# Attention and a squared-ReLU layer in one program: the first product of blocks 4 to 11 taken two blocks at a time, in a new written order

## Chip, cores and metric

One core of a Trainium2 chip runs the whole program in one launch. The metric is device time in microseconds (us). The kernel before took 197.66 us (median of 3 runs, 197.29 to 197.74).

## What is computed

The reference is local attention with a few global keys, followed by a feed-forward layer with a squared ReLU:

```
scores = (q @ k.T) / 8 - slope[h] * dist          # 4 batches, 8 heads, 768 positions, 64 wide
keep   = (key < 8) | (0 <= query - key < 96)      # 8 global keys, 96 local ones
a      = softmax(where(keep, scores, -1e9))
x      = (a @ v), heads side by side              # 3072 tokens x 512
h      = x @ w_in                                 # 512 x 2048
out    = (relu(h) ** 2) @ w_out                   # 2048 x 512
```

## The kernel before

**Tiles and blocks.** The 3072 tokens are 24 tiles of 128, numbered 0 to 23, six to a batch. Two tiles make a block, 0 to 11. The attention goes tile by tile, the feed-forward layer block by block. TensorE, VectorE, ScalarE, GpSimd and SyncE are called PE, DVE, ACT, POOL and SP, as in the profile.

**Attention of a tile j** (names as in the written order below): `load.j.1` brings q and k, `load.j.0` brings v (POOL issues them; for the tiles 0 to 5 they are single loads `ld.q.j`, `ld.k.j`, `ld.v.j`). `T.j` turns q and k: by PE (`tr`) and a copy up to tile 7, by a DMA transpose from SP from tile 8 on. `sc.j` are the scores on PE (L621). `exp.j.odd.g` are four exponentials of 128x512 on ACT (two for the first tile of a batch, L687); `mul.j.g` multiplies them by the bias on DVE (L712); `pv.j.0` and `pv.j.1` are the weighted sums of v on PE (L774); `norm.j` divides by the row sums, once for a tile, on DVE (L808, L809); `xT.j` turns the result, by PE (`trx`) up to tile 7, by a DMA transpose from SP (L894) after that.

**First product of a block** (`h`, PE, L1019). It is a Strassen-like product of seven parts, `p1` to `p7`. `xs` (DVE, L988) makes the differences of x that three of the parts need, `isum` those of w_in. Block 0 is not done so (`s1`, L1140), and of block 1 only the second half is. The parts go to three PSUM banks: x takes p1, p6, p7, p4 in this order, y takes p2, z takes p5 and p3. Between two parts on a bank its content is copied out (`u`, mostly ACT, L450) or summed and clipped at zero (`c`, DVE, L1064, or a plain ReLU on ACT, L919), since the next part adds onto the bank. `q` squares the result (ACT L1086, or DVE L1088). A part is 8 matmuls of 128 columns: four steps of the hidden dimension by two of the model dimension, and the four results fill a bank of 4x128 columns.

**Second product of a block** (`s2`, PE, L1279) is of seven parts too, each in two halves of four matmuls of 256 columns. `sum` (DVE, L1234) makes the sums of the hidden values that it needs, `wsum` (DVE, L1199) those of w_out, `part` (ACT, L450) copies between parts, `o` (DVE, L1354, or ACT) makes the output rows, and `st` stores them from SP. The second half of the first part, `s2.0.p1.1`, needs the last four of the eight loads of w_out.

**The order is written out by hand.** A string ORDER lists all operations; each engine takes its own in that order, in-order. A word names the operation, the PSUM banks or buffers that it takes (behind `:`), and at times the engine (`@A`, `@V`). Waits follow from data and from the buffers named. All loads by POOL run through one queue, in the order of the string. The constants that the change touches, and the lines that use the first of them:

```
L271      PAIRS = ()
L955          blks = (blk, blk) if mate is None else (blk, mate)
L956          wide = mate is not None
L957          GRP = 2 if wide else 4
L958          W = 2 * P if wide else P
...
                    for n, s in enumerate(range(GRP * g, GRP * g + GRP)):
                        for k in range(2):
                            nc.tensor.matmul(
                                out=tiles["h", blk, g, bank][:, n], lhsT=left_[:, s, k], rhs=right_[:, k],
...
L1120             if s == 0 and blk not in [z[0] for z in PAIRS]:
L1121                 pair = [z for z in PAIRS if z[1] == blk]
L1122                 if pair:
L1123                     first_seven(pair[0][0], mate=blk)
L1124                 else:
L1125                     first_seven(blk)
```

With `mate` given, the two halves of the tokens that the seven parts combine are the two blocks themselves instead of the two tiles of one block. A matmul then has 256 columns instead of 128, a part does two hidden steps instead of four, and there are four groups `h.b.0` to `h.b.3` for the pair instead of two for each block. `xs` takes both of its buffers for a pair, and each of its four operations is one of 128x512 values; for a block alone there is one of 128x512 and two of 128x256.

Of the kernel before, what the change touches and what calls it, by code (L numbers as in the profile page):

```python
# [57 lines left out]
tr.0.0:0 tr.1.0:1 bias.0.0:23 T.0.0 ld.q.2 tr.0.2:0 ld.q.1 tr.0.1:4 T.1.0@A sc.0.0 T.0.2 ld.k.1 tr.1.1:0 T.1.1  # L58
bias.1.0:1567 exp.0.0.0:0 ld.k.2 T.0.1@A tr.1.2:0 sc.1.0 exp.0.1.0 T.1.2 exp.1.1.0:1 gk.1 exp.1.0.1:3 exp.1.1.1
exp.1.0.0 bias.2.0:3420 sc.2.0 ld.q.3 gk.2 exp.2.1.1:2 ld.v.0 pv.0.0:56 pv.0.1 tr.0.3:7 exp.2.0.1 exp.2.0.0:0 norm.0:0  # L60
ld.v.1 ld.k.3 tr.1.3:1 T.0.3 T.1.3 pv.1.0:56 pv.1.1 exp.2.1.0 norm.1:1 sc.3.0:1372 gk.3 exp.3.1.1:3 exp.3.1.0:1
exp.3.0.0 ld.k.4 tr.1.4:4 T.1.4 exp.3.0.1 ld.q.4 tr.0.4:0 trx.0:5 T.0.4 sc.4.0:0426 exp.4.0.1:4 xT.0:0 mul.3.0:5 gv.1
exp.4.1.1 mul.3.1:1 ld.k.5 tr.1.5:1 T.1.5 exp.4.1.0:6 ld.v.2 pv.2.0:23 pv.2.1 trx.1:6 ld.q.5 tr.0.5:7 T.0.5@A gk.4
exp.4.0.0 norm.2:0 trx.2:2 gv.2 ld.v.3 pv.3.0:34 pv.3.1 sc.5.0:0715 xT.1@A ld.win.1.0 s1.0.1:6 xT.2:1 s1.0.1#2 norm.3:0
trx.3:3 ld.win.3.0 s1.0.3:4 s1.0.3#2 exp.5.1.1:1 gv.3@A ld.v.4 E0.1 ld.win.2.0 xT.3 s1.1.1:3 exp.5.0.1 exp.5.0.0:5
relu.0.3:2 mul.4.1:0 s1.0.2:0 mul.4.0:3 pv.4.0:45 pv.4.1 E0.0 exp.5.1.0 ld.win.2.1 gv.4@A relu.0.1:0 s1.0.2#2 s1.1.3:7
relu.1.3:3 sq.0.1:0 mul.5.1:6 s1.1.2:1 norm.4:0 gate.11 trx.4:4 ld.win.0.0 xT.4@A:2 ld.v.5 s1.0.0:7 ld.win.0.1 s1.0.0#2
s1.0.0#3 s1.0.2#3 mul.5.0:1 relu.1.1:0 ld.win.6.0 ld.win.7.0 isum.0.0 ld.win.5.0 xs.1.0:0 relu.1.2:5 pv.5.0:56 xs.1.1
isum.1.0 s1.0.0#4 relu.0.0:1 sq.0.3 ones.6 pv.5.1 norm.5:0 s1.0.2#4 h.2.0.p1:3 u.2.0.1:6 relu.0.2:2 sq.1.3:1 isum.2.0
sq.0.2 h.2.0.p2:1 gate.9 c.2.0.c11:4 s1.0.7:7 relu.0.7:3 isum.3.0 trx.5:5 xT.5 xs.2.0:1 ld.win.4.0 isum.0.1 xs.2.1  # L70
xs.1.2 isum.1.1 s1.0.6:6 relu.0.6:2 xs.2.2 s1.0.5:1 relu.0.5:6 h.1.1.p1:7 u.1.1.1:7 ld.wout.1 isum.3.1 h.2.1.p2:6
ld.wout.2 ld.wout.0 ld.wout.3 h.2.1.p1:5 sq.0.0 u.2.1.1:8 c.2.1.c11:1 h.1.1.p2:1 c.1.1.c11:9 sq.0.6 h.2.0.p6 u.2.0.2:a
sq.0.7 s1.0.4:0 relu.0.4@V:8 ld.wout.7 ld.wout.6 ld.wout.4 sq.0.5 isum.2.1 h.1.1.p6 u.1.1.2:3 sq.0.4 wsum.0.0 sum.0.0:0
sum.0.1 gate.12 s1.1.0:6 h.2.1.p6 u.2.1.2:6 h.2.0.p5:0 sq.1.2 h.2.0.p7 h.1.1.p7 h.1.1.p5:1 h.2.1.p7 s2.0.p2.0:4 wsum.1.0
u.2.0.3:8 h.2.0.p4 c.2.0.c22:5 u.1.1.3:7 c.1.1.c22:2 sq.1.1 u.2.1.3:b relu.1.0:8 sq.1.0 h.1.1.p4 h.2.1.p5:2 c.2.0.c21:7
wsum.2.0 c.2.1.c22:0 h.1.1.p3 c.1.1.c12:8 h.2.0.p3 ld.wout.5 wsum.0.1 wsum.2.1 wsum.1.1 h.2.1.p4 s2.0.p1.0:3 s2.0.p1.1
wsum.3.0 s2.0.p2.1 q.1.1.c22 load.6.1 tr.1.6:1 tr.0.6:6 h.2.1.p3 sum.0.2 c.2.1.c12:2 gate.10 q.1.1.c11 part.0.p1:0
load.6.0 c.1.1.c21:9 q.1.1.c12 q.2.0.c11:2 s2.0.p6.0 s2.0.p6.1 part.0.p6:1 o.0.p2:4 s2.1.p1.0:7 T.0.6@A s2.1.p1.1
q.2.0.c22 part.1.p1:0 wsum.3.1 s2.0.p7.0 s2.0.p7.1 c.2.0.c12:6 T.1.6 load.7.1 sum.0.3 s2.0.p5.0 tr.1.7:6 tr.0.7:2
s2.0.p5.1 part.0.p7:2 c.2.1.c21:5 s2.0.p4.0 s2.0.p4.1 o.0.p5:a s2.0.p3.0 s2.0.p3.1 sum.1.0:1 sum.1.1 q.2.1.c11  # L80
q.1.1.c21@V T.1.7@A sum.1.2 sum.1.3 T.0.7@A o.0.p4 q.2.0.c12 q.2.1.c12 sc.6.0:326510 exp.6.0.0:2 exp.6.1.0 s2.1.p6.0
s2.1.p6.1 mul.6.0:9 o.0.p3 part.1.p6:2 s2.1.p2.0:3 s2.1.p2.1 o.1.p2:2 s2.1.p7.0 s2.1.p7.1 load.8.1 exp.7.1.1:6 exp.7.0.1
mul.7.1:1 pv.6.0:01 pv.6.1 gk.7@A exp.7.0.0:8 s2.1.p5.0 load.7.0 s2.1.p5.1 part.1.p7:0 s2.1.p4.0 exp.7.1.0 q.2.1.c22
gate.13 load.9.1 T.8 sc.8.0:5642 exp.8.0.1:0 norm.6:0 T.9 mul.7.0:6 pv.7.0:01 pv.7.1 o.1.p5:9 s2.1.p3.0 s2.1.p3.1
exp.8.1.1 load.8.0 load.10.1 load.9.0 T.10 exp.8.0.0:1 exp.8.1.0 trx.6:4 load.11.1 xT.6@A:2 s2.1.p4.1 o.1.p4 sum.2.0:0
norm.7:1 trx.7:5 xT.7@A gk.8 o.1.p3 sc.9.0:3012 exp.9.0.0:6 h.3.1.p1:4 h.3.0.p1:7 exp.9.1.0 mul.8.1:8 mul.8.0:3 gv.7
pv.8.0:56 pv.8.1 s2.2.p1.0:3 exp.9.0.1:1 exp.9.1.1 h.3.0.p2:0 sum.2.1 xs.3.0:1 xs.3.1 norm.8:1 xT.8:1 mul.9.0:8
h.3.1.p2:1 s2.2.p1.1 mul.9.1:3 T.11 u.3.0.1:0 h.3.0.p6 sum.2.2 u.3.1.1:b h.3.1.p6 xs.3.2 c.3.1.c11:1 gk.9 part.2.p1:2
s2.2.p6.0 gv.8@A pv.9.0:56 pv.9.1 norm.9:0 xT.9 u.3.1.2:6 u.3.0.2:c s2.2.p6.1 q.2.1.c21 h.3.1.p7 u.3.1.3:5 part.2.p6:0
c.3.0.c11:b h.3.0.p7 sc.10.0:5612 exp.10.0.1:0 exp.10.1.1 exp.10.1.0:3 h.3.1.p5:0 h.3.1.p4 exp.10.0.0 u.3.0.3@V:8  # L90
h.3.0.p4 q.2.0.c21@V q.3.0.c11:1 c.3.1.c22:d h.3.0.p5:1 s2.2.p2.0:2 s2.2.p2.1 gv.9 mul.10.1:5 c.3.1.c21:0 mul.10.0:7
h.3.1.p3 s2.2.p7.0 c.3.0.c22:b c.3.1.c12:3 o.2.p2:8 c.3.0.c21:e q.3.0.c22 q.3.1.c11 load.10.0 pv.10.0:45 pv.10.1
h.4.1.p1:7 h.3.0.p3 load.12.1 gk.10@A q.3.1.c22 u.4.1.1:1 s2.2.p7.1 norm.10:1 s2.2.p5.0 sum.2.3 T.12 c.3.0.c12:d
# [72 lines left out]
def kernel(  # L166
# [98 lines left out]

    SETS = {}
    JOIN = {(7, 0), (13, 0), (19, 0)}
    COPY = []
    BEHIND = {}
    WHOLE = True  # L270
    PAIRS = ()  # L271
    NHB = 4
    NXT = 4
    SEVEN = set(range(NBLK))
    SEVEN1 = set(range(2, NBLK))
    SEVEN1_PART = {(1, 1)}
    GRP = 4
# [1221 lines left out]
```

## Time and profile before

| | |
|---|---|
| profiled execution, its own time | 197.03 us |
| its span, first to last instruction | 195.3 us |
| granted PE clock | 1.00 |
| busy in the span: PE, DVE, ACT, POOL | 188.3, 177.0, 158.6, 75.1 us |
| bytes moved by DMA | 26.92 MB |

The profile page gives busy time for each engine, a chain of the work that ended last (followed back from the last instruction to what released each step), and groups of instructions by source line. A matmul's recorded end includes the pipeline, so PE can be shown busy while it waits some tenths of a microsecond; the distance from one group of matmuls to the next in the chain is the better measure. The chain's rows have a start, a length and what ran; the timeline's rows have a start, a length, engine, line, operation, tiles, count and, in brackets, the idle time before and what ended it.

### The profile page before, as it was taken

The numbers are of one execution on the slowest core, as the hardware profiler recorded it, in microseconds if no ns is written. First come the engines' busy times: TensorE is split into PE (matmuls) and PEld (weight loads), VectorE is DVE, ScalarE is ACT, GpSimd is POOL, SyncE is SP. The second block draws the span as 40 slices with busy tenths as digits, with TensorE's granted clock in tenths as the row PEclk, the third lists the DMA queues.
The fourth block names the chain that finished last, engine by engine and source line by source line (L and its number), as shares of the span: only waits on it lengthen the run. The fifth ranks groups of instructions, "written<-read, shape, count | busy, mean of one in ns | idle before, by whom it ended". The sixth has DMA issues, their size and how long they took to land.

```text
span 195.3 us, 6863 instructions
## 1 busy us (share of the span) xinstructions
PE 188.3 (96%) x2808; PEld 171.1 (88%) x2808; DVE 177.0 (91%) x395; ACT 158.6 (81%) x331; POOL 75.1 (38%) x93
## 2 busy tenths in 40 slices
PE   7986999999999999999999999999999999999993
PEld 3865999999889989989989999998888999999882
DVE  8478999999999999999999999978999999998960
ACT  6798899999989897999997968675987979666511
POOL 8999965747575039056230009290000000000000
PEclk9999999999999999999999999999999999999999
DMA  8999999999999999999999349999855402100055
GB/s 130 149 155 174 177 201 202 204 159 158 179 159 126 147 161 191 136 240 135 142 240 84 77 91 104 198 171 206 166 104 118 134 5 57 54 3 0 0 192 187
DMA packets 111713, 26.92 MB, mean 138 GB/s; under 512 B 103234, under 2 KB 108866, under 8 KB 111682
## 3 DMA queue, kind: packets, MB, share of 16 engines
q0 software_dynamic: 80256, 13.37, 91.9%
q1 hardware_dynamic: 31426, 13.11, 32.2%
q8 instruction: 22, 0.36, 0.7%
q14 instruction: 9, 0.07, 0.1%
HBM read 27.26 MB, written 6.29 MB: 172 GB/s over the span
## 4 chain that ended last, share of the span: by engine, by line
PE 82%; DVE 10%; ACT 3%; DMA 2%; issue 1%; ACTq 0%
PE bank L1019 32%; PE bank L1279 32%; PE bank L1140 5%; PE bank L621 5%; PE bank L774 4%; DVE x L809 2%; DVE hsum L1234 2%; DMA xT<-x 2%; PE bank L393 2%; DVE buf L712 2%; PE bank L531 2%; ACT early L687 1%; ACT buf L687 1%; DVE xs L988 1%; DVE early L712 1%
## 5 line engine op out<-in xcount | busy, mean ns | idle before, releaser
L1279 PEld LDWEIGHTS <-hsum 128*128 128x128 bf16 x384 | 35.9, 98 | 3.9
L450 ACT COPY buf<-bank 128x512 f32<-128x512 f32 (+1 forms) x56 | 30.8, 564 | 10.0 <-PE bank L1019 5.8
L1279 PE MATMUL bank<-wsum,hsum 128*128 128x256 bf16 x288 | 37.7, 273 | 0.0
L687 ACT ACTIVATE buf<-bank 128x512 bf16<-128x512 f32 x54 | 30.1, 604 | 2.3 <-PE bank L621 2.3
L1019 PEld LDWEIGHTS <-qk_first 128*128 128x128 bf16 x504 | 30.7, 98 | 1.4 <-DVE xs L988 0.3
L1086 ACT ACTIVATE hs<-buf 128x512 bf16<-128x512 f32 x46 | 28.7, 636 | 3.5 <-DVE buf L1064 3.2
L1019 PEld LDWEIGHTS <-win 128*128 128x128 bf16 x504 | 30.8, 98 | 0.8
L1064 DVE CUSTOM_DVE_ANT_0 buf<-bank,buf 128x512 f32<-128x512 f32 x42 | 28.3, 684 | 1.8 <-ACT early L687 0.7
L1279 PEld LDWEIGHTS <-hs 128*128 128x128 bf16 x288 | 26.7, 98 | 2.7
L331 POOL DMA_DIRECT2D qk<-in_q_dram x18 | 16.0, 889 | 30.1 <-DMA qkT<-qk 25.7
L1279 PE MATMUL bank<-wout,hs 128*128 128x256 bf16 x192 | 26.0, 273 | 0.0
L1019 PE MATMUL bank<-xT,win 128*128 128x128 bf16 x336 | 24.3, 219 | 0.0
L1019 PE MATMUL bank<-xs,qk_first 128*128 128x128 bf16 x336 | 24.1, 219 | 0.2 <-DVE xs L988 0.2
L331 POOL DMA_DIRECT2D v<-in_v_dram x18 | 16.1, 898 | 20.5 <-DVE hsum L1234 14.3
L687 ACT ACTIVATE early<-bank 128x512 bf16<-128x512 f32 x34 | 19.2, 612 | 2.8 <-PE bank L621 2.7
L809 DVE TENSOR_TENSOR x<-bank,rs 128x512 bf16<-128x512 f32 x24 | 16.6, 692 | 0.9
L331 POOL DMA_DIRECT2D qk<-in_k_dram x18 | 16.2, 898 | 2.3 <-DMA wout<-in_moe_w_out_dram 2.3
L1234 DVE TENSOR_TENSOR hsum<-hs 128x1024 bf16<-128x1024 bf16 (+1 forms) x26 | 16.7, 643 | 0.0
L450 ACT COPY part<-bank 128x256 f32<-128x256 f32 x31 | 11.6, 376 | 5.8 <-PE bank L1279 5.6
L1354 DVE TENSOR_TENSOR buf<-bank,part 128x256 f32<-128x256 f32 x29 | 12.1, 419 | 3.6 <-PE bank L1279 3.3
L621 PEld LDWEIGHTS <-qkT 64*128 64x128 bf16 x352 | 10.0, 94 | 3.9 <-issue 2.6
L1279 PE MATMUL bank<-wout,hsum 128*128 128x256 bf16 x96 | 13.3, 273 | 0.0
(93 smaller groups left out, 379.8 us busy)
## 6 DMA issues: line engine op xcount, KB each, us to landing
out_dram<-buf SPq DMA_DIRECT2D x17, 256.0 KB, 2.5
v<-in_v_dram POOLq DMA_DIRECT2D x24, 128.0 KB, 5.6
qk<-in_q_dram POOLq DMA_DIRECT2D x18, 128.0 KB, 4.8
qk<-in_k_dram POOLq DMA_DIRECT2D x18, 128.0 KB, 5.4
wout<-in_moe_w_out_dram POOLq DMA_DIRECT2D x8, 256.0 KB, 10.2
win<-in_moe_w_in_dram POOLq DMA_DIRECT2D x6, 256.0 KB, 6.7
out_dram<-early SPq DMA_DIRECT2D x5, 256.0 KB, 2.8
qk_first<-in_q_dram POOLq DMA_DIRECT2D x5, 128.0 KB, 4.4
```

The lines of the kernel that those rows point to most:

```text
L331: nc.gpsimd.dma_start(out=dst, in_=src)
L450: nc.scalar.copy(dst, src)
L621: nc.tensor.matmul(out=tiles["sc", j, odd, g][:, at, :], lhsT=left[j - 1][half, pair, :] if kt else qkT[j % NKT][half, 1, pair, :], rhs=qk ...
L687: nc.scalar.activation(out=tiles[tag, j, g][:, odd], in_=tiles.pop(("sc", j, odd, g)).rearrange("p a c -> p (a c)"), func=Act.Exp, scale=s ...
L809: nc.vector.tensor_tensor(out=x.rearrange("p (b a) c -> p b a c", b=2), in0=po[:, :, :, :D], in1=rs.to_broadcast([P, 2, 4, D]), op=Alu.mult,)
L1019: nc.tensor.matmul(out=tiles["h", blk, g, bank][:, n], lhsT=left_[:, s, k], rhs=right_[:, k], start=opens and n == 0 and k == 0, stop=k == ...
L1064: nc.vector._custom_dve(TENSOR_ADD_SAT, out=hr, in0=src, in1=tiles.pop(("u", blk, g, i)), s0=float("inf"), s1=0.0,)
L1086: nc.scalar.activation(hs, hr, Act.Square)
L1140: nc.tensor.matmul(out=hT[:, c, cols], lhsT=w_in_sb[s][:, kt, c * P : (c + 1) * P], rhs=tiles["xT", blk][:, kt, cols], start=(kt == 0), st ...
L1234: nc.vector.tensor_tensor(out=t[:, i, h], in0=t[:, a, h] if isinstance(a, int) else half_a(blk, *a)[:, h], in1=t[:, b, h] if isinstance(b, ...
L1279: nc.tensor.matmul(out=tiles["acc", blk, bank][:, cols], lhsT=left_[:, s], rhs=right_[:, cols], start=first and s == 0, stop=s == NSTEP - ...
L1354: nc.vector.tensor_tensor(out=o_sb[:, cols], in0=tiles["acc", blk, bank][:, part], in1=tiles["part", blk, other][:, part], op=Alu.add,)
```

## The change

Two things change: the constant PAIRS, and the whole ORDER string. PE transposes up to tile 7 and one normalisation for a tile stand in both kernels.

```diff
-    PAIRS = ()
+    PAIRS = ((4, 5), (6, 7), (8, 9), (10, 11))
```

Of the string, the line before and the line after at the place where block 0 begins its second product:

```diff
-sum.0.1 gate.12 s1.1.0:6 h.2.1.p6 u.2.1.2:6 h.2.0.p5:0 sq.1.2 h.2.0.p7 h.1.1.p7 h.1.1.p5:1 h.2.1.p7 s2.0.p2.0:4 wsum.1.0
+exp.6.1.0 h.2.0.p3 exp.7.0.1:2 c.2.0.c12:b h.2.0.p2:1 s2.0.p1.0:7 exp.7.1.1 exp.7.1.0 h.2.0.p4 c.2.0.c21:8 ld.wout.7 T.8
```

**PE, the first part of the first product of block 4.** Before, 128 columns to a matmul (`xT_107` is the turned x of block 4, `win` the weights):

```order
L1019 LDWEIGHTS win
L1019 MATMUL bank<-xT_107,win 128x128
L1019 LDWEIGHTS win
L1019 MATMUL bank<-xT_107,win 128x128
L1019 LDWEIGHTS win
L1019 MATMUL bank<-xT_107,win 128x128
```

Now:

```order
L1019 LDWEIGHTS win
L1019 MATMUL bank<-xT_107,win 128x256
L1019 LDWEIGHTS win
L1019 MATMUL bank<-xT_107,win 128x256
L1279 LDWEIGHTS hsum_114
L1279 MATMUL bank<-wsum_91,hsum_114 128x256
```

Each weight load now serves 256 columns, four in a part instead of eight, and a part of block 2's second product follows.

**POOL, the queue of loads, from the last loads of w_in on.** `qk_67` to `qk_69` are the q and k of the tiles 6, 8 and so on, `v_77` is the v of tile 6. Before:

```order
L327 DMA win<-in_moe_w_in_dram 128x4x256 x4
L327 DMA wout<-in_moe_w_out_dram 128x2x512 x8
L331 DMA qk_67<-in_q_dram 128x8x64
L331 DMA qk_67<-in_k_dram 128x8x64
L331 DMA v_77<-in_v_dram 128x8x64
```

Now:

```order
L331 DMA qk_67<-in_q_dram 128x8x64
L331 DMA qk_67<-in_k_dram 128x8x64
L327 DMA win<-in_moe_w_in_dram 128x4x128 x2
L327 DMA win<-in_moe_w_in_dram 128x4x256
L331 DMA qk_69<-in_q_dram 128x8x64
L331 DMA qk_69<-in_k_dram 128x8x64
L327 DMA wout<-in_moe_w_out_dram 128x2x512
L331 DMA qk_68<-in_q_dram 128x8x64
L331 DMA qk_68<-in_k_dram 128x8x64
L327 DMA wout<-in_moe_w_out_dram 128x2x512 x3
L331 DMA qk_67<-in_q_dram 128x8x64
L331 DMA qk_67<-in_k_dram 128x8x64
```

Behind these stand the last four loads of w_out and then `v_77`:

```order
L327 DMA wout<-in_moe_w_out_dram 128x2x512 x4
L331 DMA v_77<-in_v_dram 128x8x64
L331 DMA qk_68<-in_q_dram 128x8x64
L331 DMA qk_68<-in_k_dram 128x8x64
L331 DMA v_78<-in_v_dram 128x8x64
```

Eight loads, q and k of the tiles 6, 8, 7 and 9, have moved ahead of the last loads of w_out; the v of tile 6 stands behind all of them as it did behind w_out before.

**ACT, around the first exponentials of tile 6** (L687 are exponentials, `part` the copies between parts of the second product, `hs` the squares). Before:

```order
L450 COPY part_129<-bank 128x256
L919 ACTIVATE buf_122<-bank 128x512
L1086 ACTIVATE hs_111<-buf_121 128x4x128
L1086 ACTIVATE hs_112<-buf_117 128x4x128
L450 COPY part_130<-bank 128x256
L450 COPY qkT_86<-bank 128x512
L1086 ACTIVATE hs_112<-buf_118 128x4x128
L450 COPY part_129<-bank 128x256
L450 COPY part_131<-bank 128x256
```

Now:

```order
L1176 ACTIVATE hs_111<-early 128x512 x2
L687 ACTIVATE early<-bank 128x512 x6
L919 ACTIVATE buf_121<-bank 128x512
L687 ACTIVATE buf_120<-bank 128x512
L1086 ACTIVATE hs_111<-buf_118 128x4x128
L687 ACTIVATE buf_120<-bank 128x512
L687 ACTIVATE buf_118<-bank 128x512
L450 COPY part_129<-bank 128x256
```

Nine exponentials of the tiles 6 to 8 now stand ahead of the first copy of the second product (`part_129`). Before, the four copies shown (`part_129` twice, `part_130`, `part_131`) stood ahead of the first exponential of tile 6, which came some rows behind them.

206 lines of the change are left out of this document (103 added, 103 removed).

## Prediction

> **What bounds the kernel now.** I read the page first, then the chain of waits in order of time, the stages of the span, and the queue of loads.
>
> ```profile
> PE 188.3 (96%) x2808; PEld 171.1 (88%) x2808; DVE 177.0 (91%) x395; ACT 158.6 (81%) x331; POOL 75.1 (38%) x93
> ...
> PE 82%; DVE 10%; ACT 3%; DMA 2%; issue 1%; ACTq 0%
> ```
>
> PE carries 82% of the chain, but DVE and ACT have little to spare. Where they have least, the stages show (columns: PE, PEld, DVE, ACT, POOL busy, clock, DMA, GB/s):
>
> ```profile
> 10.00:20.00 10.00, 7.71 (x165) 6.22 (x164) 8.04 (x23) 8.64 (x19) 10.00 (x14) 1.00 2.13 165
> ...
> 20.00:58.30 38.30, 38.30 (x564) 35.49 (x561) 37.82 (x83) 36.29 (x76) 25.59 (x32) 1.00 1.81 181
> ...
> 170.00:180.00 10.00, 10.00 (x131) 9.38 (x129) 9.23 (x18) 7.27 (x16) 0.00 (x0) 1.00 0.06 23
> ```
>
> Up to 20 us everything still waits for the first loads. From 20 to 58.3 us three engines are full together: DVE idles 0.48 us (38.30 - 37.82) and ACT 2.01 us. Later ACT has over a quarter to spare. The chain says the same: from 47 to 64.5 us it runs through DVE, after that through PE almost alone.
>
> ```profile
> 47.78 0.41 DVE buf L1354
> ...
> 56.99 0.01 DVE early L1354
> ...
> 60.98 1.20 DVE buf L712 x2
> ...
> 64.56 0.62 PE bank L621 x16
> ...
> 77.60 1.34 PE bank L1019 x24
> ...
> 179.82 12.24 PE bank L1279 x112
> 192.08 0.37 ACT buf L450
> ```
>
> So what shortens PE's work counts only if nothing puts PE later in the first 60 us; and what puts it later there is not won back, because behind that PE has no idle time to win it from.
>
> **The change, term by term.** The sum is made against the profiled execution, 197.03 us (span 195.3 us and 1.73 us around it). It stands 0.63 us below the median of the runs, 197.66 us, and I add that at the end.
>
> *PE's work.* A part of the first product is 8 matmuls of 128 columns now and 4 of 256 afterwards. The chain has both back to back: 24 of 128 in 1.34 us, 55.8 ns each, 0.447 us a part; 112 of 256 in 12.24 us, 109.3 ns each, 0.437 us a part. Four pairs by four groups by seven parts are 112 parts: 112 x 0.0095 = **-1.06 us**. All of it is on the path, since PE is. The halved weight loads (448 fewer) take nothing off besides, since they lie beside the matmuls.
>
> ```profile
> L1019 PEld LDWEIGHTS <-win 128*128 128x128 bf16 x504 | 30.8, 98 | 0.8
> ```
>
> A load lasts 98 ns by itself, and yet 128-column matmuls follow one another every 55.8 ns. The Trainium skill (TensorE: Matmul & The Clock Gate, Back-to-back issue gap) gives some 81 ns for a sustained stream of weight loads and 128-column matmuls. By that price a part of eight would be 0.65 us and the change would take off some 24 us, an estimate from that section; the chain's 55.8 ns speaks against it, and the sum goes by the chain.
>
> *xs on DVE.* For two blocks alone it is two of 128x512 and four of 128x256, for a pair four of 128x512.
>
> ```profile
> L988 DVE TENSOR_TENSOR xs<-xT,xs 128x256 bf16<-128x256 bf16 x22 | 6.2, 284 | 0.3
> L988 DVE TENSOR_TENSOR xs<-xT 128x512 bf16<-128x512 bf16 x11 | 4.6, 419 | 0.3 <-DMA xT<-x 0.3
> ```
>
> 4 x 0.419 against 2 x 0.419 + 4 x 0.284: 0.30 us less a pair, 1.2 us in all. It falls behind 58 us, where DVE is not what PE waits for, so I cost it at nothing. If DVE were still the bound there, it would be a gain of up to 1.2 us. The copies, sums and squares keep their number and size; DVE gives four squares to ACT, hidden in ACT's idle time late in the span.
>
> *The first 60 us in the new order.* The first product of block 4 now needs the tiles 8 to 11 and not 8 and 9, so attention is pulled ahead of the second products. Three floors follow, and the highest counts.
>
> (a) *Loads.* In the order of before, the last load of w_out is issued at 30.48 us; the queue is full, each issue waiting for a landing.
>
> ```profile
> 26.44 0.70 POOL L327 DMA_DIRECT2D wout<-in_moe_w_out_dram  x1 [0.52 <-DMA win<-in_moe_w_in_dram]
> ...
> 30.48 0.71 POOL L327 DMA_DIRECT2D wout<-in_moe_w_out_dram  x1 [0.67 <-DMA win<-in_moe_w_in_dram]
> DMA to landing us min/median/max: 8.9/10.2/10.8
> q0 software_dynamic: 10893, 1.38, 217.0%
> L331 POOL DMA_DIRECT2D v<-in_v_dram x18 | 16.1, 898 | 20.5 <-DVE hsum L1234 14.3 <-DVE v L501 6.2
> ```
>
> The third row is that of w_out's tile: it lands at 39.4 to 41.3 us. The fourth is the queue from 40 to 50 us: 1.38 MB in 10 us, so 128 KB take 0.95 us; by POOL's own row an issue is 0.90 us. Eight loads of q and k now stand ahead, and the v of tile 6 follows: nine by 0.90 to 0.95 make that v land at 47.5 to 49.9 us, middle 48.7. PE's first use of it is the weighted sum of tile 6, which before ran here:
>
> ```profile
> 52.76 0.41 PE L774 MATMUL bank<-v,buf 128*128 128x65 bf16 x8
> ...
> 57.86 1.07 PE L1019 MATMUL bank<-xT,win 128*128 128x128 bf16 x16
> ```
>
> Counted in both orders, the work of PE ahead of it is the same but for 16 halves of second products fewer (16 x 0.437 = 6.99 us) and one group of scores more (0.62 us, the 16 matmuls of L621 in the chain above). PE would come to it at 52.76 - 6.37 = 46.4 us. It waits **1.1 to 3.5 us**, middle 2.3. In-order, everything of PE is queued behind it: the rest of blocks 0 and 1's second products and the scores of tile 9, and ACT and DVE behind these.
>
> (b) *ACT.* A place with the same work of PE ahead of it in both orders (to 0.2 us) is the first part of block 3. Before, it is the second half of the row at 57.86, at 58.3 us. Ahead of it ACT must now have done 39 exponentials instead of 32, and with the smaller differences 3.4 us more:
>
> ```profile
> 14.49 0.99 ACT early L687 x2
> ...
> 57.51 0.43 ACT L450 COPY buf<-bank 128x256 f32<-128x256 f32 x1
> ```
>
> 7 x 0.50 us are 3.5; the rest cancels. The copy at 57.51 us is ACT's last operation that this place needs, in both orders. With all 2.01 us of idle time used, it comes at 57.51 + 3.4 - 2.0 = 58.9 us and lasts 0.43 us, so the place is at 59.3 us; without waits PE would be there at 58.1 us, having 0.2 us less to do. The floor is **+1.2 us**.
>
> (c) *DVE.* Ahead of the same place it must do 13 multiplications by the bias instead of 9, two squares and a normalisation more, some sums fewer: 2.4 us more at 0.60 us (the pair at 60.98 in the chain is 1.20). Its last needed operation ended at 57.0 us before (the chain's row at 56.99). With its 0.48 us of idle used, the last multiplication ends at 58.9 us, and a wait and a weighted sum on PE (0.4 us, eight matmuls as at 52.76) come before the place: 59.3 us again, **+1.2 us**.
>
> None of the floors adds to another, since ACT and DVE work on while PE waits. I take **+2.1 us**: near the middle of (a), and above (b) and (c), which allow ACT and DVE no idle time at all. Bounds 0.8 (floors a third too high, early loads) and 3.5.
>
> *Waits of PE that go.* Before, PE still waits behind 60 us: the scores at 64.56 us follow DVE in the chain, and between 140 and 150 us there is a wait for the turned x of block 10.
>
> ```profile
> 60.00:70.00 10.00, 9.91 (x175) 9.45 (x173) 9.90 (x23) 9.44 (x20) 3.71 (x5) 1.00 1.78 164
> ...
> 140.00:150.00 10.00, 9.84 (x164) 8.81 (x162) 9.46 (x22) 8.54 (x20) 0.00 (x0) 1.00 0.62 139
> ```
>
> 0.09 + 0.16 us by busy time, which hides some of each. A PE that is 1 us later finds both ready: **-0.3 us**, bounds -0.6 and +0.5 (new waits on the pairs, whose four tiles must be there together). The tail is the same: second products alone, ACT's copy at 192.08 us, and 3.2 us for the last store.
>
> Sum: -1.06 + 2.1 - 0.3 = **+0.7 us**, 197.03 to 197.8; with 0.63 for the median, **198.4 us**.
>
> **The rivals.**
>
> *Faster: the loads come early enough.* If the v of tile 6 lands before 47.2 us, PE waits under 0.8 us for it; and if ACT and DVE need a third less than I count, the stage costs 0.8. Then -1.06 + 0.8 - 0.4 = -0.7: 197.0. It decides below a stage cost of 1.0 us. For it: the shortest landing of w_out, 8.9 us, and that PE's own order may let it do more before the waits. Against it: two floors of 1.2 that do not depend on loads.
>
> *No change: the floors alone count.* The stage costs 1.4 us: -1.06 + 1.4 - 0.3 = 0.0, 197.7.
>
> *Much slower: DMA transposes take from the loads.* The transposes of the tiles 8 and 9 are now due before 48 us; before, the first began at 46.7 us. Both use the engines that the loads fill.
>
> ```profile
> L557 SPq DMA_TRANSPOSE qkT<-qk x16: 1232/1303/1941, 46.7 to 145.4; - x16
> q1 hardware_dynamic: 3338, 1.04, 58.1%
> ```
>
> From 60 to 70 us SP's queue moved 1.04 MB in 5.8 us of all engines' time; 256 KB are 1.46 us. Two of them put the v of tile 6 off by 0 to 2.9 us; with half, 1.5 us more: 199.9. The Trainium skill (DMA: Bandwidth & Descriptors, Issuing engines are not separate DMA queues) says that DMAs of SP and POOL run on the same engines and interleave, which would make it nearer 2.9 than 0; no row of before has a transpose while w_out loads.
>
> *Weight loads that are not hidden.* Were every load of 98 ns on the path, a part of eight would be 0.78 us and one of four still 0.44. The chain has 0.447 for eight. Were a third of the difference real in the blocks 4 to 11, 112 x 0.11 = 12 us would go: 185. The skill's 81 ns above points this way.
>
> **How the numbers follow.** Forecast 0.40 (own range 198.1 to 199.3), faster 0.21, no change 0.23, transposes 0.15, unhidden weight loads 0.01. A measurement of this kernel can tell about 0.2%, 0.4 us. Faster by more: 0.22; within: 0.23; slower by more: 0.55. The range leaves out the ends of the faster and the much slower case: 196.9 to 200.0.
>
> **What would show it.** Right: 256-column parts at 0.437 us; PE idle 1 to 3.6 us ahead of the weighted sum of tile 6, released by the load of v, at 47 to 50 us; the first part of block 3 at 59.5 to 61 us; almost no wait of PE behind that. Wrong: that weighted sum before 47.5 us, or ACT and DVE with idle time between 20 and 58 us while PE does not wait; or a wide part that costs more than 0.44 us, or new waits of PE on the turned x of a pair behind 60 us.

## The result and the profile after

The changed kernel takes 209.06 us (median of 4 runs, 205.98 to 211.08) against 197.56 us: ratio **1.048**, interval 1.039 to 1.058. Measured again later it was 208.68 us (6 runs), ratio 1.046 (1.040 to 1.052). The prediction said 198.4 us, with a range that ended at 200.0. Its direction came true, its size was off by more than 10 us. Its first mechanism came true in part: PE does wait for POOL's queue near 50 us, but 2.33 us of that wait are for w_out and only 0.42 us for the v of tile 6, on which the prediction had put all of it. Medians here are over all runs; the ratios leave out runs more than 1.5% above a kernel's fastest.

The profiled execution took 209.88 us, span 208.1 us. First the page's engine row, its clock row, and the first row of its chain of waits:

```profile
PE 191.4 (92%) x2360; PEld 165.4 (79%) x2360; DVE 176.7 (85%) x387; ACT 157.9 (76%) x331; POOL 75.1 (36%) x93
...
PEclk9799999999699999999999999999999999999999
...
PE 59%; DMA 23%; DVE 6%; ACT 3%; POOL 3%; issue 3%; SPq 1%; DVEq 0%; POOLq 0%
```

The 448 matmuls fewer are there (2808 to 2360). But DMA, 2% of the chain before, is now 23%, PE's share fell from 82 to 59%, and the clock dips twice. The stages that the prediction read, now in the changed kernel (PE, PEld, DVE, ACT, POOL busy, clock, DMA share, GB/s):

```profile
20.00:58.30 38.30, 34.27 (x525) 30.50 (x525) 34.79 (x77) 33.82 (x69) 25.65 (x32) 0.96 1.87 167
60.00:70.00 10.00, 9.32 (x139) 8.27 (x137) 9.07 (x21) 9.03 (x23) 4.18 (x5) 1.00 2.00 132
140.00:150.00 10.00, 9.59 (x120) 8.45 (x120) 9.81 (x21) 7.55 (x17) 0.00 (x0) 1.00 0.41 95
170.00:180.00 10.00, 10.00 (x94) 8.96 (x92) 9.04 (x18) 8.33 (x17) 0.00 (x0) 1.00 0.15 54
```

From 20 to 58.3 us, where three engines were full together before, PE, DVE and ACT now idle 4.0, 3.5 and 4.5 us: none of them is the bound there any more. The longest steps of the chain say what is (start, length, what; DMA rows are transfers):

```profile
38.62 2.77 POOL wout L327 x4
41.38 13.29 DMA v<-in_v_dram
56.23 8.24 DMA qkT<-qk
...
90.09 7.48 DMA out_dram<-buf
...
119.12 7.94 DMA out_dram<-buf
...
133.18 5.36 DMA xT<-x
```

The v of tile 6 takes 13.3 us to land, a DMA transpose of q and k (qkT) 8.2 us, output stores 7.5 and 7.9 us. PE does not wait for a store itself: in the chain DVE does, for a buffer that the store still reads, and PE for DVE. These are PE's own waits for transfers, with the idle time and its releaser in brackets:

```profile
8.00 0.61 PE L531 MATMUL bank<-ident,qk_first 128*128 128x128 bf16 x4 [1.74 <-DMA qk_first<-in_q_dram]
...
52.52 1.86 PE L1279 MATMUL bank<-wout,hs 128*128 128x256 bf16 x8 [2.33 <-DMA wout<-in_moe_w_out_dram]
54.81 0.60 PE L774 MATMUL bank<-v,buf 128*128 128x65 bf16 x8 [0.42 <-DMA v<-in_v_dram]
...
64.52 0.23 PE L621 MATMUL bank<-qkT 64*128 64x128 bf16 x2 [0.68 <-DMA qkT<-qk]
...
67.75 0.61 PE L1019 MATMUL bank<-xT,win 128*128 128x128 bf16 x8
```

The row at 54.81 is the weighted sum of tile 6, forecast at 47.5 to 49.9 us; the last row is the first part of block 3, forecast at 59.5 to 61 us and at 58.3 us before. Behind it some 4.5 us more are lost, where no wait was forecast: the span is 12.8 us longer, 9.4 of them by then, so the rest is 3.4 us longer, although PE has 1.1 us less of work there. Two of these waits cost more than their idle time (same columns as the stages):

```profile
4.00:8.00 4.00, 2.18 (x15) 1.24 (x13) 2.20 (x8) 2.46 (x8) 4.00 (x5) 1.00 1.91 158
8.00:12.00 4.00, 4.00 (x42) 2.92 (x44) 0.00 (x0) 1.26 (x3) 4.00 (x6) 0.58 2.40 155
48.00:52.00 4.00, 2.19 (x32) 1.65 (x30) 3.70 (x7) 3.52 (x8) 3.03 (x4) 1.00 1.61 182
52.00:56.00 4.00, 3.05 (x21) 2.04 (x21) 1.14 (x3) 2.18 (x5) 1.75 (x2) 0.57 2.08 154
```

Each time, after a stretch in which PE was busy for only 2.2 of 4 us, its clock was at half for about 3.4 us ((1 - 0.57) x 4 / 0.5). At half clock 3.4 us do the work of 1.7. The mean clocks of the runs, 0.975 to 0.992, come to one to three such stretches. That is part of the reach of 206 to 211 us, but not all of it: a run at 0.981 took 205.96 us and one at 0.975 took 208.25 us.

What fills the queue at the decisive time is one view: the DMA queues from 40 to 45 us (packets, MB, their time as a share of all 16 engines). The kernel before:

```profile
q0 software_dynamic: 6081, 0.77, 241.5%
```

The changed kernel:

```profile
q0 software_dynamic: 2043, 0.31, 161.2%
q1 hardware_dynamic: 643, 0.16, 69.2%
```

q0 carries POOL's loads, q1 SP's transposes and stores. The transpose of tile 8 now runs here, and the loads move 0.31 MB in the 5 us instead of 0.77. A load's packets are about as large as before (0.77 MB / 6081 = 127 bytes; 0.31 / 2043 = 152), but the recorded time of one is twice as long: 2.415 x 16 x 5 us / 6081 = 32 ns, then 1.612 x 16 x 5 / 2043 = 63 ns. (Shares above 100% show that packets' times overlap; they are not time for which one packet has an engine to itself.) The 5 us are a mean of two parts. From 40 to 43 us, where the transpose runs, q1 has 620 packets with a share of 114%, and the loads move 0.07 MB; from 44 to 45 us, where it has ended, they move 0.15 MB in that 1 us, as before.

### The profile page after: what moved, and what is told of

It is laid out like the page before. It is cut to its first block, busy times and chain, and to the rows that moved or that the text cites. A ratio compares the mean times of both kernels' runs of the same rounds, so it can differ in the third digit from the quotient of the medians.

```text
span 208.1 us, 5964 instructions
## 1 busy us (share of the span) xinstructions
PE 191.4 (92%) x2360; PEld 165.4 (79%) x2360; DVE 176.7 (85%) x387; ACT 157.9 (76%) x331; POOL 75.1 (36%) x93
## 3 DMA queue, kind: packets, MB, share of 16 engines
q1 hardware_dynamic: 31426, 13.11, 34.9%
## 4 chain that ended last, share of the span: by engine, by line
PE 59%; DMA 23%; DVE 6%; ACT 3%; POOL 3%; issue 3%; SPq 1%; DVEq 0%; POOLq 0%
PE bank L1279 27%; PE bank L1019 19%; DMA out_dram<-buf 7%; DMA v<-in_v_dram 6%; PE bank L774 4%; DMA qkT<-qk 4%; PE bank L1140 3%; PE bank L621 3%; DMA qk_first<-in_q_dram 3%; DMA xT<-x 3%; DVE buf L1064 2%; ACT early L687 1%; POOL wout L327 1%; PE bank L600 1%; DVE buf L712 1%
## 5 line engine op out<-in xcount | busy, mean ns | idle before, releaser
L1086 ACT ACTIVATE hs<-buf 128x512 bf16<-128x512 f32 x61 | 37.5, 636 | 9.0 <-DVE buf L1064 6.1
L687 ACT ACTIVATE buf<-bank 128x512 bf16<-128x512 f32 x62 | 34.7, 615 | 5.8 <-PE bank L621 5.0
L450 ACT COPY buf<-bank 128x512 f32<-128x512 f32 (+1 forms) x54 | 28.0, 558 | 4.6 <-DVE buf L1064 1.4
L1064 DVE CUSTOM_DVE_ANT_0 buf<-bank,buf 128x512 f32<-128x512 f32 x40 | 26.9, 683 | 3.1 <-DMA out_dram<-buf 1.6
L1019 PEld LDWEIGHTS <-qk_first 128*128 128x128 bf16 x312 | 25.6, 98 | 4.3 <-issue 1.6
L1019 PEld LDWEIGHTS <-win 128*128 128x128 bf16 x312 | 25.8, 98 | 3.4 <-issue 1.1
L1019 PE MATMUL bank<-xs,qk_first 128*128 128x256 bf16 (+1 forms) x208 | 24.2, 252 | 0.9 <-DVE buf L1064 0.9
L1019 PE MATMUL bank<-xT,win 128*128 128x256 bf16 (+1 forms) x208 | 24.2, 252 | 0.2 <-ACT early L687 0.2
L712 DVE TENSOR_TENSOR buf<-buf,E 128x1024 bf16<-128x1024 bf16 x23 | 15.6, 681 | 1.4 <-DMA out_dram<-buf 0.7
L687 ACT ACTIVATE early<-bank 128x512 bf16<-128x512 f32 x26 | 14.0, 617 | 3.1 <-PE bank L621 3.0
```

Of the source, the lines that this page charges most:

```text
L450: nc.scalar.copy(dst, src)
L687: nc.scalar.activation(out=tiles[tag, j, g][:, odd], in_=tiles.pop(("sc", j, odd, g)).rearrange("p a c -> p (a c)"), func=Act.Exp, scale=s ...
L712: nc.vector.tensor_mul(at, tiles.pop(("esc", j, g)), bias)
L1019: nc.tensor.matmul(out=tiles["h", blk, g, bank][:, n], lhsT=left_[:, s, k], rhs=right_[:, k], start=opens and n == 0 and k == 0, stop=k == ...
L1064: nc.vector._custom_dve(TENSOR_ADD_SAT, out=hr, in0=src, in1=tiles.pop(("u", blk, g, i)), s0=float("inf"), s1=0.0,)
L1086: nc.scalar.activation(hs, hr, Act.Square)
```

## The experiments

Differences in us are of medians, to the changed kernel at 208.7 us or to the kernel named; where the ratios give another size, both are said. In the diffs of the order only the words moved are shown.

| kernel | median us | ratio to before (95% interval) |
|---|---|---|
| the changed kernel, second time | 208.68 | 1.046 (1.040 to 1.052) |
| old_start | 214.07 | 1.085 (1.080 to 1.091) |
| new_start | 208.76 | 1.056 (1.052 to 1.060) |
| win_later | 209.36 | 1.054 (1.049 to 1.060) |
| copy_8_11 | 204.71 | 1.027 (1.020 to 1.034) |
| v6_first | 211.50 | 1.065 (1.059 to 1.070) |
| copy_win | 204.00 | 1.026 (1.020 to 1.032) |
| copy_lru | 206.61 | 1.034 (1.025 to 1.043) |
| before_copy | 198.16 | 1.002 (0.999 to 1.005) |
| copy_all | 200.00 | 1.010 (1.006 to 1.014) |
| before_copy_all | 197.63 | 0.999 (0.997 to 1.002) |
| copy_all_128 | 201.14 | 1.014 (1.010 to 1.018) |
| copy_12_on | 205.00 | 1.036 (1.032 to 1.039) |
| copy_all_win | 199.54 | 1.008 (1.005 to 1.011) |
| copy_all_win_v6 | 204.43 | 1.033 (1.029 to 1.036) |
| before_load8 | 201.38 | 1.018 (1.015 to 1.021) |
| before_load8_T | 201.10 | 1.017 (1.014 to 1.021) |
| before_load8_copy | 200.22 | 1.008 (1.005 to 1.012) |

### Which half of the order: old_start and new_start

```diff
 old_start (PAIRS on)
+ORDER = the 436 words of before ahead of block 4's first product, then the words left, as in after
 new_start (PAIRS = ())
+ORDER = the 459 words of after ahead of block 4's first product, then the words left, as in before
```

Where a buffer or bank was still in use at the seam, another free one was taken.

> The order of the kernel before up to the first product of block 4 (436 words), then everything that is left in the order of the changed kernel, with the blocks 4 to 11 in pairs. Theory A, the loss lies in the early order and the late waits of PE (4.2 us more than before behind 65 us) only follow from it: 197.6 - 1.06 for the wide parts, less or more 0.5, so 196 to 197.5 us. Theory B, the late waits belong to the new late order itself, whose operations wait for buffers that output stores still hold: 197.6 - 1.06 + 4.2 = 200.7, between 199.5 and 202 us.

> The complement: the order of the changed kernel up to the first product of block 4 (459 words), then the rest in the order of before, one block at a time. Theory A (all of the loss is early): 197.6 + 10.3 = 207 to 210 us. Theory B (4.2 us belong to the late order): 197.6 + 9.3 - 0.6 = 205 to 207 us. Both expect PE idle for about 4 us near 50 to 55 us and two stretches of 3.4 us at half clock.

new_start took 208.76 us: the early order alone, without a single pair, costs as much as the whole change. That fits theory A in its total. Its trace has a reserve: the first part of block 3 stands at 67.61 us, 9.3 us later than before, and behind it 2.1 us more are lost in the old late order, half of them in a wait of 1.1 us at 83 us, near its seam. old_start took 214.07 us and fits neither theory. At the seam the exponentials of the tiles 10 and 11 that the old beginning had left over come in a row, and PE waits 1.4 us at 72.9 us; then it waits for DVE, 2.8 us at 87.8 us and 3.1 us at 98.5 us, and in the chain each of these follows a store of 5.6 us. The run does not tell whether the seam or the later order makes these waits, and it prices nothing. "Pairs alone" was priced in another way, below.

### The start: win_later

```diff
-exp.1.0.0:1 ld.win.4.0 bias.0.0:32
+exp.1.0.0:1 bias.0.0:32
-ld.v.3 T.0.4
+ld.v.3 ld.win.4.0 T.0.4
```

> The changed kernel with one load moved: the half load of w_in that is third in its order of loads is issued behind the v of tile 3. Theory C, the start stands on the path: PE's idle 1.74 us at 8 us goes, and with it the 3.41 us at half clock that follow (1.7 us): 3.4 us faster, about 205.5 us. Theory D, the w_out and v loads near 54 us decide whatever PE does before: under 1 us faster, 208 to 209 us, with PE idle near 50 to 55 us for 3 us longer.

209.36 us, nothing won: theory D. PE's wait for tile 1 shrank from 1.74 us to 0.38 and 0.45, and its wait for w_out near 52 us grew from 2.3 to 3.6 us; the load that was moved makes PE wait 1.2 us at 26.4 us. PE came to the parts that need w_out 0.9 us earlier all the same, and could go on 0.3 us later. What PE does ahead of w_out doesn't count while w_out comes late.

### The transposes of the tiles 8 to 11: copy_8_11 and its control

```diff
-nc.sync.dma_start_transpose(out=T_.rearrange("p n a c -> p (n a) c"), in_=qk_ring[slot(j)]...)
+if 8 <= j <= 11: nc.sync.dma_start(out=T_.rearrange("p n a c -> p (n a c)"), in_=qk_ring[slot(j)]...)
+else: nc.sync.dma_start_transpose(...)
```

> The changed kernel with the DMA transposes of q and k of the tiles 8 to 11 replaced by plain copies of the same 256 KB each (so these tiles' scores are computed on data that is not turned). Theory E, the transposes take the engines from the loads (from 40 to 45 us the queue of loads moved 0.31 MB where before moved 0.77 MB): w_out and the v of tile 6 land 2.5 to 3.5 us earlier, the scores of tile 10 do not wait: 3.5 to 5 us faster, about 204.5 us. Theory F, the loads are late because POOL's queue stands behind loads that wait for PE (2.35, 0.92 and 2.55 us idle from 34 to 47 us): under 1 us faster, 208 to 209 us.

> A control: the kernel before, with plain copies in place of the DMA transposes of the tiles 8 to 11. Theory E (a transpose costs only where loads that PE will wait for are in flight): none of its transposes runs while w_out loads, PE waits for nothing in that stage, so within 0.5 us of before, 197.2 to 198 us. If the copies made any order faster by themselves: 2 us or more faster than before.

204.71 us, 4.0 us faster than the changed kernel, and the same edit leaves the kernel before as it was (198.16 us, ratio 1.002). Theory E. The queues from 40 to 45 us with the copies:

```profile
q0 software_dynamic: 2684, 0.85, 154.0%
q1 hardware_dynamic: 86, 0.15, 8.2%
```

About the same bytes of q and k are moved, in 86 packets instead of 643 and with an eighth of the share, and the loads move 0.85 MB. (These 5 us hold more of w_out, whose packets are larger, so 0.85 MB is not the same mix as the 0.77 MB of before; from 40 to 43 us the loads move 0.45 MB beside the copy and 0.07 MB beside the transpose.) By the ratios the gain is 3.8 us. PE's wait for w_out is down to 0.63 us, and tile 6's weighted sum starts at 51.5 instead of 54.8 us:

```profile
50.67 1.03 PE L1285 MATMUL bank<-wout,hs 128*128 128x256 bf16 x8 [0.63 <-DMA wout<-in_moe_w_out_dram]
...
51.54 0.41 PE L780 MATMUL bank<-v,buf 128*128 128x65 bf16 x8
```

### POOL's queue: v6_first

```diff
-ld.wout.0 ... load.9.1 sc.6.0 ... ld.wout.7 T.8 ld.wout.6 sc.8.0 ... T.9 ... ld.wout.5 ld.wout.4 ... load.6.0
+ld.wout.0 ... sc.6.0 ... ld.wout.7 T.8 ld.wout.6 sc.8.0 ... ld.wout.5 ld.wout.4 ... load.6.0 load.9.1 T.9
```

> The changed kernel with the load of q and k of tile 9 (and its DMA transpose) moved behind the last four loads of w_out and the v of tile 6, so that these no longer stand in POOL's queue behind a load that waits for PE (2.35 us at 34.5 us). Theory F (the queue's order): w_out and that v land 4 to 6 us earlier, PE's idle 2.3 and 0.4 us near 52 to 55 us and the half-clock stretch behind them go: 3 to 5 us faster than the changed kernel, 204 to 206 us. Theory E (the DMA transpose of tile 8, which still runs then): they land 1 to 2 us earlier, and the later q, k and transpose of tile 9 give it back: 207.5 to 210 us.

211.50 us, 2.8 us slower: theory F falls as a remedy. The waits for w_out and v are gone, and one longer wait stands in their place, at the scores of tile 9:

```profile
59.45 0.29 PE L621 MATMUL bank<-qkT 64*128 64x128 bf16 x2 [8.15 <-DMA qkT<-qk]
```

The new order needs w_out, the v of tile 6 and the q and k of tile 9 within 5 us of one another; whichever comes last is waited for.

### What is left after the copies: copy_win and copy_lru

```diff
 copy_win: copy_8_11 with the edit of win_later
 copy_lru: copy_8_11 with
-c.4.3.c22:a ... st.6.1 ... u.10.0.2:a
+every :digit of an f32 buffer, from h.3.0.p1 on, is that of the buffer free longest
```

> The kernel with plain copies in place of the DMA transposes of the tiles 8 to 11 (204.7 us), and the half load of w_in that was third in the order of loads behind the v of tile 3 besides. By itself this edit moved the changed kernel by nothing (209.4 against 209.1 us), while PE then waited 1.4 us longer for w_out. If w_out's landing hides what the start is worth, then with the transposes gone most of the start shows: 2 to 3 us faster than with the copies alone, 202 to 203 us. If the start is worth nothing in itself (the load only makes PE wait elsewhere, at 26 us): 204 to 206 us.

> The kernel with plain copies for the tiles 8 to 11, and from the first product of block 3 on every operation takes the f32 buffer that has been free longest, in place of the one named in the table (194 words get another number; no order changes). Theory B', PE's late waits (0.8 to 1.1 us each at 85 to 123 us) come from buffers that an output store still holds for 7 to 8 us: they go, 2 to 3 us faster than the copies alone, about 202 us. Rival, the stores are late whatever buffer is taken, and all buffers are in use: within 1 us of 204.7.

204.00 and 206.61 us, against 204.71, with intervals that overlap its own: neither the start nor this choice of buffers shows a gain. Stores still took 6 to 7 us in copy_lru and were waited for with other buffers.

### All transposes: copy_all, its control and its complement

```diff
 copy_all, before_copy_all: nc.sync.dma_start in place of nc.sync.dma_start_transpose for every T.j and xT.j (j >= 8)
 copy_12_on: the same, but T.8 to T.11 stay transposes
```

> The changed kernel with every DMA transpose (q and k of the tiles 8 to 23, x of the tiles 8 to 23) replaced by a plain copy of the same bytes; what is computed on them is not turned. Theory E', transposes that take the DMA engines from loads and stores make all of the loss but the start: PE's late waits go too, 197.6 - 1.06 + up to 2 for the start = 196.5 to 199 us. Rival G, the rest of the loss (6 to 7 us after the copies of the tiles 8 to 11) lies in the order itself, in queues and buffers: 201 us or more.

> Control: the same replacement in the kernel before. PE has no waits to lose but about 1 us behind 60 us: 197 to 198 us. If plain copies freed DVE or ACT of something in any order: 196 or less.

> The complement of the copies for the tiles 8 to 11: the changed kernel with those four transposes kept, and the transposes of q and k of the tiles 12 to 23 and of x replaced. Theory E': the early loss stays, the late waits go: 2 to 4 us faster than the changed kernel, 205 to 207 us. Rival G: within 1.5 us of it, 208 to 210 us.

copy_all took 200.00 us: **8.7 of the 11 us are gone**, and nothing in the control (197.63 us). By the ratios it is 7.1 of 9.1 us. The two parts add up to most of it: the tiles 8 to 11 4.0 us, all others 3.7 us (3.8 and 2.1 us by the ratios). The traces, one execution of each kernel, tell where. The mark is the first part of block 3:

| kernel | mark, us | from the mark to the end of the span, us |
|---|---|---|
| before | 58.3 | 137.0 |
| changed kernel | 67.75 | 140.35 |
| copy_8_11 | 63.31 | 139.1 |
| copy_12_on | 67.07 | 136.0 |
| copy_all | 62.78 | 135.6 |
| before_copy_all | 59.06 | 136.8 |

The rows of the mark in copy_8_11, copy_12_on and copy_all:

```profile
63.31 0.61 PE L1025 MATMUL bank<-xT,win 128*128 128x128 bf16 x8
...
67.07 0.61 PE L1025 MATMUL bank<-xT,win 128*128 128x128 bf16 x8
...
62.78 0.61 PE L1019 MATMUL bank<-xT,win 128*128 128x128 bf16 x8
```

Without the transposes of the tiles 8 to 11 the mark comes 4.4 us earlier, up to 1.7 us of it the stretch at half clock behind PE's wait for w_out. Without all the others the mark stays within 0.7 us, and the rest is 4.3 us shorter. So the late loss, which copy_lru did not touch, comes from transposes as well: the later ones. Theory E', but 1 us above the range it gave. The median time from issue to landing in the changed kernel:

```profile
out_dram<-buf SPq DMA_DIRECT2D x20, 256.0 KB, 2.9
...
v<-in_v_dram POOLq DMA_DIRECT2D x24, 128.0 KB, 7.7
...
qkT<-qk SPq DMA_TRANSPOSE x16, 7.5
xT<-x SPq DMA_TRANSPOSE x16, 5.5
```

and in copy_all:

```profile
out_dram<-buf SPq DMA_DIRECT2D x20, 256.0 KB, 2.7
qkT<-qk SPq DMA_DIRECT2D x16, 256.0 KB, 4.9
v<-in_v_dram POOLq DMA_DIRECT2D x24, 128.0 KB, 6.5
...
xT<-x SPq DMA_DIRECT2D x16, 128.0 KB, 2.6
```

A transpose that lands late also holds one of three q and k buffers: the next load waits for it, and with it all that POOL issues behind. These waits of POOL, in the changed kernel (total, times, longest; 25.7 us in 7 waits before):

```profile
POOL qk L331 <- DMA qkT<-qk: 43.5, 9, 8.2
```

and in copy_all:

```profile
POOL qk L331 <- DMA qkT<-qk: 33.2, 9, 7.4
```

So the copies act in two ways, through the engines' time and through these buffers; no run here takes them apart.

### The rest: copy_all_win and copy_all_win_v6

```diff
 copy_all_win: copy_all with the edit of win_later
 copy_all_win_v6: and load.9.1, T.9 behind load.6.0, as in v6_first
```

> The changed kernel with every DMA transpose as a plain copy (200.0 us), and the half load of w_in that was third among the loads behind the v of tile 3. If the start makes the rest: 2 us faster, 197.5 to 198.5 us. If PE's waits near 44.5 and 50 us (1.2 and 1.3 us, for DVE and for w_out) set the place and take up what the start wins: within 0.7 us of 200.0.

> The same, and the q and k of tile 9 (load and copy) behind the last four loads of w_out and the v of tile 6. If w_out's place in the queue makes the rest of the rest: PE's 1.3 us near 50 us go and the time is 1 to 1.5 us below that of the kernel with the start alone edited, 197 to 199 us. If the scores of tile 9 then wait in their place (their wait was 8.3 us with the transposes): as much or more slower.

199.54 us: the start shows 0.5 us, within the intervals, for PE still waits for DVE and for w_out. In copy_all:

```profile
44.50 0.61 PE L1019 MATMUL bank<-xT,qk_first 128*128 128x128 bf16 x8 [1.03 <-DVE buf L1064]
46.97 0.21 PE L621 MATMUL bank<-qkT 64*128 64x128 bf16 x1 [0.15 <-DVE buf L1064]
49.90 1.03 PE L1279 MATMUL bank<-wout,hs 128*128 128x256 bf16 x8 [1.13 <-DMA wout<-in_moe_w_out_dram]
```

The first of these waits, for DVE, is in part one for w_out as well: DVE's operation stands behind two sums of w_out, and DVE itself idled 0.52 us until w_out had landed:

```profile
42.43 0.69 DVE L1199 TENSOR_TENSOR wsum<-wout 128x1024 bf16<-128x1024 bf16 x1 [0.52 <-DMA wout<-in_moe_w_out_dram]
```

copy_all_win_v6 took 204.43 us: with the q and k of tile 9 put behind, their scores wait 4.2 us. What is left is thus of the kind of the prediction's floor (a), late loads, with w_out and not the v of tile 6 as the one that is waited for, and the one change of POOL's queue that was run here put a longer wait in its place.

### The wide parts alone: copy_all_128

```diff
-nc.tensor.matmul(out=tiles["h", blk, g, bank][:, n], lhsT=left_[:, s, k], rhs=right_[:, k], ...)
+for c in range(0, W, P): nc.tensor.matmul(out=...[:, n, c : c + P], lhsT=left_[:, s, k], rhs=right_[:, k, c : c + P], ...)
```

> As the changed kernel with all transposes replaced, and each 256-column matmul of the first product of the blocks 4 to 11 given as two of 128 columns (896 matmuls in place of 448). The prediction's term for PE's work, 112 x 0.0095 = 1.06 us: 1.0 to 1.2 us slower than with 256 columns, if PE's work is what counts there; nothing, if waits hide it; 20 us or more slower, if 128-column matmuls with a weight load each cost the 81 ns that the Trainium skill (TensorE: Matmul & The Clock Gate, Back-to-back issue gap) gives.

201.14 against 200.00 us, +1.1 by the medians and +0.8 by the ratios, whose intervals overlap: in line with the prediction's -1.06 us for PE's work, though the two times alone do not measure it, and far from 20 us. The parts in the chains show it, at 0.01 us a part. In copy_all_128, parts of eight:

```profile
175.51 0.45 PE bank L1020 x8
...
177.26 0.45 PE bank L1020 x8
```

In the changed kernel, parts of four:

```profile
169.07 0.44 PE bank L1019 x4
...
176.06 0.44 PE bank L1019 x4
```

### One transpose among the loads of w_out: before_load8, before_load8_T, before_load8_copy

```diff
 before_load8
-h.1.1.p1:7 u.1.1.1:7 ld.wout.1
+h.1.1.p1:7 u.1.1.1:7 load.8.1 ld.wout.1
 before_load8_T: and T.8 right behind load.8.1
 before_load8_copy: before_load8, and T.8 a plain copy
```

> The kernel before with one move: the load of q and k of tile 8 is issued ahead of the first load of w_out; its transpose stays in its place in the order. PE uses w_out at 41.4 us, when it has just landed (39.4 to 41.3 us), and two loads more stand ahead of it at 0.90 to 0.95 us each: 0.5 to 1.9 us slower than before, 198.3 to 199.7 us.

> The same, and the DMA transpose of tile 8 right behind that load, so that it runs while w_out loads. Nothing waits for it early. Theory E (one 256 KB transpose among the loads puts them off by 2.5 to 3.5 us): 2 to 3.5 us slower than with the load alone, 200.5 to 203 us, with PE idle ahead of the first second products near 41 to 46 us. Rival (a transpose takes only what 256 KB take, or the loads' queue is not the limit): within 1.4 us of the kernel with the load alone.

> The kernel before with the load of q and k of tile 8 ahead of w_out, and the transpose of tile 8 (which then runs from 32.8 us, among the loads of w_out) replaced by a plain copy. Theory E: the early load alone costs 0.5 to 1.9 us (two loads of 0.90 to 0.95 us ahead of w_out), so 198.4 to 199.8 us, and the transpose was the other 1.5 to 3 us of 201.3. Rival: the load alone makes the 3.4 us, 200.7 to 201.7 us.

The first two, 201.38 and 201.10 us, don't differ, and the reason is a fault of the pair: SP has nothing else to do then, so the transpose ran from 32.8 us in both, and in both it was in flight for about 12 us. It wasn't the rival that won; the comparison was empty. The third can tell: ratio 1.008 against 1.018, so the early load costs 1.7 us and the transpose 1.8 us more, inside E's 1.5 to 3. With both intervals taken into account that is 0.9 to 2.7 us; the medians are 1.2 us apart. In before_load8 PE waits in two places:

```profile
45.37 0.92 PE L1279 MATMUL bank<-wout,hs 128*128 128x256 bf16 x7 [1.04 <-DMA wout<-in_moe_w_out_dram]
47.05 0.62 PE L531 MATMUL bank<-ident,qk 128*128 128x128 bf16 x8 [0.76 <-DMA qk<-in_k_dram]
```

With the copy both waits are gone. Its trace, of an execution of 202.9 us, one of the longest of its twelve, has another wait instead, 2.35 us for DVE at 44.4 us; before_load8_T has 1.3 us of that kind too, before_load8 none. So the price of a single transpose is rough.

## Why the prediction was wrong, step by step

**PE's work, -1.06 us: right as far as it can be measured.** Parts of eight run in 0.45 us and parts of four in 0.44, and copy_all_128 was 1.1 us slower by its median. The weight loads were hidden; the 12 us of the rival with unhidden loads are excluded, and so are the 24 us by 81 ns a matmul.

**The first 60 us, +2.1 us (bounds 0.8 to 3.5): this step failed.** Measured at its own mark, the first part of block 3, it was 67.75 - 58.3 = 9.4 us with 0.2 us less of PE's work ahead. That is 7.3 us more than the 2.1. Two things in it were wrong: some 5 us are the first (67.75 - 62.78, the mark without any transpose) and 2.4 us the second.

The first is the rate in floor (a): "128 KB take 0.95 us", taken from 40 to 50 us of before, a stretch in which no transpose ran while w_out loaded. With the transpose of tile 8 in flight the loads moved 0.31 MB in 5 us, some 2 us for 128 KB, and the v of tile 6 landed at 54.7 us instead of 48.7. PE came there some 4 us late too (at 50.2 us to the second product just ahead of it, instead of 46.4); that its wait, 2.33 + 0.42 us, lies within the 1.1 to 3.5 is luck. Without the transposes of the tiles 8 to 11 the mark stands at 63.31 us, 4.4 us earlier.

The second is that the highest floor alone should count. Without any transpose the mark still stands at 62.78 us, 4.5 us later than before (3.7 us later than in the control), and that is above the upper bound of 3.5. In copy_all PE idles 0.65 us more than before in the first 20 us, which the sum left out, then waits 1.03 us for DVE at 44.5 us (half of it w_out's lateness) and 1.13 us for w_out at 49.9 us, and these add up. About 3.1 us of the 4.5 show as idle time of PE; the rest stays open.

**The transposes: listed as a rival, and mis-sized.** It had the right mechanism and the right place, a chance of 0.15, and +1.5 us for two transposes. The row I priced it by (1.04 MB in 5.8 us of all engines' time, from 60 to 70 us) mixes transposes with stores and x, and I took it as time of the engines that the loads only have to share out. The runs showed 1.8 us for one transpose (before_load8 against its copy), 4.0 us for four, and 3.7 us for all the others (2.1 us by the ratios), which the rival had at nothing. The Trainium skill (DMA: Bandwidth & Descriptors, Issuing engines are not separate DMA queues) says that both queues interleave on the same engines. The rows of 40 to 45 us agree that they share them (loads at 0.31 instead of 0.77 MB beside 0.16 MB of transposes); from 40 to 43 us the loads got very little of them.

**Waits that go, -0.3 us, and "almost no wait of PE behind that": wrong in the changed kernel.** Some 4.5 us were lost behind the mark. I had reasoned that a later PE finds everything ready. But the transfers were later than PE: loads, transposes and stores wait for one another through three q and k buffers and 16 f32 buffers. Without transposes the term comes out: from the mark on copy_all takes 135.6 us and the kernel before 137.0, 1.4 us less, where -1.06 and -0.3 give 1.36. That it comes so close, with one execution of each, is partly luck.

**Left out: the first 20 us and the clock.** The new order of the first loads made PE wait 1.74 us at 8 us, and I said nothing of it; in the changed kernel it cost nothing in the end, because PE then waited less for w_out (win_later). The clock's half stretches I hadn't counted either: up to 1.7 us each, one to three in a run. A reading was too broad besides: ACT has over a quarter to spare only from 170 to 180 us; behind 58.3 us it is 22% on the whole, and 15% from 140 to 150 us.

**Floors (b) and (c), ACT and DVE:** not the last to come in the changed kernel's long waits ahead of the mark. Once the transposes are gone a wait for DVE shows, 1.03 us at 44.5 us, but at a sum (L1064) behind those of w_out, and not at the multiplication by the bias that (c) named.

What stays open: how the price of a transpose divides between the engines' time and the buffers that it holds, and by which way the later transposes make stores late. No run gave a version below the kernel before: without transposes the changed kernel is still 2.4 us slower than its control, so the order costs about 3.5 us and the wide parts give back 1.1.

## What to carry to other kernels

A rate of a queue read in one stage holds only for what else ran in that stage: when an order moves a DMA transpose into the stretch in which a full queue feeds the bound engine, price it from a row in which both run together, or give it a wide bound upward. A schedule that leaves three engines full has no slack to absorb late data, so look first at what lands last, and only then at the engines' sums. And when a move within a queue is to be tested, see first what the queue does there: in an empty queue an instruction runs where its data lands, not where its word stands.

## What the runs showed of the hardware

- A DMA transpose of bf16 data is dear in packets and in their time on the engines, and not in bytes: 0.16 MB in 643 packets had a share of 69% of 16 engines over 5 us, about the same bytes as a plain copy 86 packets and 8%. Over the whole kernel the 32 transposes as copies cut SP's queue from 31426 to 16578 packets and from 34.9 to 21.1% of the engines' time, with the same 13.11 MB.
- While the transpose of tile 8 ran, from 40 to 43 us, the loads moved 0.07 MB; beside a plain copy of the same tile they moved 0.45 MB.
- PE's clock fell to half for 3.4 us, twice in one execution, after a stretch in which PE was still busy for 2.2 of 4 us. The Trainium skill (TensorE: Matmul & The Clock Gate, Part 1: The HAM clock gate) gives half rate and windows of about 3.4 us, which agrees; it asks for a whole idle window, and here idle stretches of 1.7 and 2.3 us were enough.
- 128-column matmuls, each with a weight load of its own, cost 55.8 to 56 ns in a row and not the 81 ns of the Trainium skill (TensorE: Matmul & The Clock Gate, Back-to-back issue gap): twice as many of half the width, 448 more, made 1.1 us in 200.
